# RWKV-7 state update and quick-GELU MLP: another form of the triangular inverse for the first four units

## The chip, the core and the metric

The kernel runs on one core of one Trainium2 chip. The metric is the device time in microseconds of one execution. Five engines work side by side: TensorE (PE in the profile; PEld is its loading of stationary operands), VectorE (DVE), ScalarE (ACT), GpSimd (POOL) and SyncE (SP), which here issues all transfers. Each takes its own instructions in their program order and waits for the others by semaphores.

## The reference

Two blocks follow one another. The first is a recurrence over 768 steps, for 4 batches and 8 heads of 40 channels, with one 40 x 40 state for each batch and head:

```python
for t in range(S):
    y[:, :, t] = np.einsum('bhd,bhde->bhe', rt, state)
    Sa = np.einsum('bhde,bhe->bhd', state, at)
    state_decay = state * wt[:, :, None, :] - np.einsum('bhd,bhe->bhde', Sa, bt)
    state = state_decay + np.einsum('bhd,bhe->bhde', vt, kt)
```

Its output, rearranged to 3072 tokens of 320 values, goes through an MLP: `h = x @ w_in` (320 to 2048), `g = h * sigmoid(1.702 h)`, `g @ w_out` (2048 to 320). All is fp32.

## The kernel before, in words

The 768 steps are cut into 12 chunks of 64 tokens. A unit is one chunk of two of the four batches, 16 batch-heads, so there are 24 units; units 2c and 2c+1 make chunk c. Within a unit the 64 steps become matrix products (`prep`, `inverse`, `solve`), and only the state goes on from unit i to unit i+2. When both units of a chunk are done, the chunk's MLP (`mlp`) can run: 40 groups of ps_up, four activations g, 2 x 8 groups of ps_down, and the stores. The output x of a unit goes to DRAM and back (`part_with`, `get_back`) to be rearranged.

The in-chunk dependence needs T, the inverse of I + N for a strictly triangular 64 x 64 matrix N for each batch-head. `inverse` makes it so. `score_N` computes N in PSUM. The two 32 x 32 diagonal blocks are inverted by five levels of matmuls with a doubling of powers; then two products, ps_Q and ps_T, add the off-diagonal block (`off_one`, `off_two`, with P21, QT and Tc), and T goes into `solve` (ps_X, M, ps_y). Partitions hold two blocks of 64 rows; the four 64 x 64 quarters of TensorE work as independent tiles, and a level is 16 matmuls with a 64 x 64 stationary operand each.

In the form of before a level n has these steps: E (the current power plus the identity, 32 columns for each of eight tiles) is turned by a 32 x 32 transpose on VectorE to ES (L648); ES is spread by a mask `quads` into EX (L655, or in two halves on ScalarE, L653), a block diagonal of two 32 x 32 blocks, which serves as stationary operand; the matmuls multiply EX with W, whose first 32 columns are two times the identity minus E and whose last 32 are the running product; the result is copied to the next W (L684), and two times the identity minus its first half gives the next E (L686). For level 0, E comes from N by two predicated copies onto an identity (L637, one for each diagonal block), and W's first half by a subtraction (L643); the identities in E0 and W0 are set once at the start (L373). After the last level one more transpose and spread make T.

The MLP's weights come as eight pieces of 1280 columns in a 64-bit form: 0 to 3 are w_in, 4 to 7 w_out. Each piece takes a transfer, one ScalarE step (L413) and five VectorE steps (L417, L421, L422, L425, L429). Some are staged in a buffer `extra` of two places, so that piece 4's transfer waits for the end of piece 0, that of 5 for 3, of 6 for 4 and of 7 for 5. ps_up needs pieces 0 to 3; ps_down parts 2k and 2k+1 need piece 4+k.

No loop sets the order of the instructions. Every step is a task of `Plan` with a rank, the engines that may run it with an assumed duration for each, what it reads and writes, and the buffers and PSUM pairs (four, of two banks each) that it takes. `Plan.order` goes through an assumed time line, gives each free engine the able task of the lowest rank, and so decides both engine and place of every instruction; `Plan.paced` does this four times with shifted release times for the MLP's tasks and keeps the order with the earliest assumed end. The tasks are then issued in that order. So a change of some tasks moves many others. MLP tasks have ranks from 10000, units have ranks of ten per unit.

Of the kernel before, what the change touches and what calls it, by code (L numbers as in the profile page):

```python
# [22 lines left out]
ALU = mybir.AluOpType  # L23
ACT = mybir.ActivationFunctionType
# [201 lines left out]
def rwkv7_gelu_quick(ctx: ExitStack, tc: tile.TileContext, time_d, v_d, w_d, wc_d, ak_d, b_d, rv_d, w_in, w_out, out):  # L226
    nc = tc.nc
# [10 lines left out]
    LEVELS = 5  # L238
    WALK = "ebufbub"
    EARLY = 4  # L240
    BY_PE = 4
    ROUNDS, WINDOW, SHARE = 4, 5000.0, 1.0
    RANKS = [14, 16, 20, 24, 35, 37, 39, 41]
    HALF = [slice(0, 64), slice(64, 128)]
    BITS = (0, 1)
# [6 lines left out]
    banks = ctx.enter_context(tc.tile_pool(name="banks", bufs=1, space=bass.MemoryType.PSUM))  # L252

    plan = Plan(dict(logw=3, wc=3, G=1, wch=3, wz=2, time=2, ak=2, b=2, rv=2, FT=3, GT=1, kh=2, bh=2, zr=2, rz=2,
                     A=1, B=1, RV=2, E0=2, W0=2, P21=2, W=2, E=2, ES=2, EX=2, T=2, Tc=1, QT=1, zraw=2, zT=1, M=2, x=1, xT=3, g=4, ob=1), 4)
    tiles, psums, drams = {}, {}, {}

    def single(name, shape):
# [9 lines left out]
    def psum(t, name):  # L268
        if t.pair not in psums:
            psums[t.pair] = banks.tile([128, 2, 512], FP32, tag=f"pair{t.bank}", name=name)  # L270
        return psums[t.pair]

    def mm(o, lhsT, rhs, start):
        nc.tensor.matmul(o, lhsT, rhs, start=start, stop=True, skip_group_check=True)  # L274
# [338 lines left out]
    def turn(i, n, of):  # L613
        return of * 2 * (i // 2) + i % 2 + 2 * n


    def inverse(i):
# [17 lines left out]
        plan.add(R, pe((4, 64)), score_N, reads=T("ahT", "bhT") + ([("preset", 1)] if i == 1 else []), uses=T("ak", "b"), room=T("E0", "P21"), pair=("N", i))  # L635
        for n in BITS:
            plan.add(R, dve(256), lambda t, n=n: nc.vector.copy_predicated(  # L637
                tiles_of(at(E0_t, i)), every(within_of(n), [128, 2, 4, 32]), blocks(psum(t, ""), 64)[:, :, :, 32 * n:32 * n + 32]),
                     writes=T("E0"), pair=("N", i))
        plan.add(R, any2(256), lambda t: copy(t.engine)(  # L640
            at(P21_t, i)[:, :256].rearrange("p (r j t) -> p r j t", r=2, t=32), blocks(psum(t, ""), 64)[:, :, :, :32]),
                 writes=T("P21"), pair=("N", i))
        plan.add(R, {"DVE": 430.0, "POOL": 750.0, "sbuf": True}, lambda t: of(t.engine).tensor_sub(  # L643
            at(W0_t, i)[:, :, :32], two32.unsqueeze(1).to_broadcast([128, 8, 32]), at(E0_t, i)), reads=T("E0"), writes=T("W0"))

        def turned(rank, source, reads, n, dst, writes):

            plan.add(rank, dve(256), lambda t: nc.vector.transpose(ES(n), source(t)), writes=[key("ES", n, 6)], **reads)  # L648

            def spread(t):  # L650
                if t.engine == "ACT":
                    for h in BITS:
                        nc.scalar.activation(dst[:, :, h], ES(n), ACT.Copy, scale=quads[:, h, :1])  # L653
                else:
                    of(t.engine).tensor_mul(dst, ES(n).unsqueeze(2).to_broadcast([128, 8, 2, 32]),  # L655
                                            quads.unsqueeze(1).to_broadcast([128, 8, 2, 32]))
# [12 lines left out]
        def level(n):  # L669
# [18 lines left out]
                     writes=[key("E", n + 1, 5)], pair=pair)  # L688
            turned(rank, lambda t: E(n + 1), dict(reads=[key("E", n + 1, 5)]), n + 1, EX(n + 1), [key("EX", n + 1, 5)])

        for n in range(LEVELS):
# [336 lines left out]
```

## Time and profile before

| | |
|---|---|
| median of 3 runs | 734.87 us (731.48 to 738.36) |
| profiled execution | 741.96 us, its span 740.3 us |
| mean granted TensorE clock | 0.959 |
| PE busy | 679.0 us, 92% of the span |
| DVE busy | 445.9 us, 60% |
| ACT busy | 343.8 us, 46% |
| POOL busy | 214.5 us, 29% |
| moved by DMA | 69.80 MB, mean 94 GB/s |

A line of a group or of the timeline names the engine, the line of the kernel and the operation, then the written and read tiles with their shapes. All matmuls are issued in a helper at L274, so they are told apart by their PSUM tile: ps_level is a level of the inverse, ps_up and ps_down are the MLP. The trace counts each fp32 matmul twice. Times in square brackets are the engine's idle time before the line, with what ended it.

### The profile page before, as it was taken

To read this page: it belongs to the slowest core of one execution; us is meant where nothing else is said; L and a number is where in the kernel's file an instruction comes from. 1 tells how busy PE (TensorE), PEld (TensorE's weight loads), DVE (VectorE), ACT (ScalarE), POOL (GpSimd) and SP (SyncE) were. 2 spreads that over 40 slices of the span, in tenths; PEclk is the share of its full clock that TensorE was granted. 3 is DMA by queue.
4 is the path that set the end of the run, shared out by engine and by line. 5 is a ranking of instruction groups with operands and counts; after the bars stand their busy time and mean duration, and the time that the engine had idled before them with its cause. 6 is when DMAs were issued, how large, how long until landed. Compare 5 with 4: busy or idle time off the path is not lost.

```text
span 740.3 us, 43272 instructions
## 1 busy us (share of the span) xinstructions
PE 679.0 (92%) x20096; PEld 560.7 (76%) x20096; DVE 445.9 (60%) x795; ACT 343.8 (46%) x666; POOL 214.5 (29%) x279
## 2 busy tenths in 40 slices
PE   4575895899999999999999999999999999999997
PEld 3465773687888977887887888988888798777564
DVE  5788798878558566666557467656666546542000
ACT  4555465445535535545645526445446345332120
POOL 7236124243323333322322233422441421200000
PEclk9576699899999999999999999999999999999999
DMA  7951544243251242341332233341331230110000
GB/s 227 350 177 53 168 139 148 65 117 107 57 169 47 77 122 73 87 136 49 99 102 71 74 95 104 98 120 55 99 101 50 83 93 4 40 48 29 13 9 19
DMA packets 31860, 69.80 MB, mean 94 GB/s; under 512 B 5056, under 2 KB 14272, under 8 KB 30656
## 3 DMA queue, kind: packets, MB, share of 16 engines
q1 hardware_dynamic: 31680, 67.03, 30.1%
q8 instruction: 158, 2.59, 1.5%
q14 instruction: 22, 0.18, 0.1%
HBM read 59.15 MB, written 7.86 MB: 91 GB/s over the span
## 4 chain that ended last, share of the span: by engine, by line
PE 77%; DVE 7%; ACT 5%; DMA 5%; issue 2%; POOL 2%; SPq 2%; DVEq 0%; POOLq 0%; ACTq 0%
PE ps_down L274 25%; PE ps_up L274 25%; PE ps_level L274 7%; PE ps_y L274 4%; PE ps_B L274 4%; PE ps_X L274 2%; PE ps_T L274 2%; PE ps_Q L274 2%; DMA ak<-in_ak 1%; PE ps_rz L274 1%; DVE ES L648 1%; PE ps_N L274 1%; PE ps_RV L274 1%; PE ps_A L274 1%; DMA extra<-in_w_out 1%
## 5 line engine op out<-in xcount | busy, mean ns | idle before, releaser
L274 PE MATMUL ps_up<-xT,w_sb 64*64 64x256 f32 x3840 | 251.3, 379 | 2.7 <-DVE RV L605 1.5
L274 PE MATMUL ps_down<-w_sb,g 64*64 64x320 f32 x3072 | 246.6, 436 | 4.9 <-DVE w_sb L429 2.5
L274 PEld LDWEIGHTS ps_up<-xT,w_sb 64*64 64x64 f32 x3840 | 152.7, 134 | 32.0 <-DVE RV L605 1.6
L274 PEld LDWEIGHTS ps_down<-w_sb,g 64*64 64x64 f32 x3072 | 135.6, 135 | 50.3 <-issue 7.6
L274 PEld LDWEIGHTS ps_level<-W,EX 64*64 64x64 f32 x3840 | 85.3, 141 | 41.6 <-ACT EX L653 14.3
L274 PE MATMUL ps_level<-W,EX 64*64 64x64 f32 (+1 forms) x3840 | 87.4, 226 | 26.6 <-ACT EX L653 11.6
L653 ACT ACTIVATE EX<-ES,quads 128x256 f32<-128x256 f32 x120 | 54.5, 501 | 59.7 <-DVE ES L648 57.5
L684 ACT COPY W<-ps_level 128x512 f32<-128x512 f32 x67 | 39.3, 586 | 71.5 <-PE ps_level L274 71.2
L882 ACT ACTIVATE g<-ps_up 128x1024 f32<-128x1024 f32 x48 | 49.1, 1024 | 42.5 <-PE ps_up L274 42.2
L686 DVE TENSOR_TENSOR E<-two,ps_level 128x256 f32<-128x256 f32 x96 | 39.7, 413 | 48.1 <-ACT W L684 48.0
L655 POOL TENSOR_TENSOR EX<-ES,quads 128x512 f32<-128x512 f32 x26 | 37.7, 1449 | 80.3 <-DVE ES L648 57.6
L648 DVE STREAM_TRANSPOSE ES<-E 128x256 f32<-128x256 f32 x120 | 53.2, 444 | 5.6
L582 POOL TENSOR_TENSOR kh<-time,G 128x320 f32<-128x320 f32 x22 | 19.7, 894 | 123.9 <-PE ps_y L274 72.1
L908 DVE TENSOR_TENSOR ob<-ob,ps_down 128x320 f32<-128x320 f32 x24 | 11.6, 485 | 63.4 <-ACT ob L906 63.0
L785 ACT COPY B<-ps_B 128x416 f32<-128x416 f32 x41 | 20.6, 507 | 62.4 <-PE ps_B L274 62.4
L847 POOL TENSOR_TENSOR x<-zr,FT 128x128 f32<-128x128 f32 x80 | 42.7, 563 | 5.4 <-DVE zr L837 3.4
L643 POOL TENSOR_TENSOR W<-two,E 128x256 f32<-128x256 f32 x22 | 16.1, 731 | 95.5 <-DVE E L637 95.5
L274 PE MATMUL ps_y<-M,bh 64*64 64x104 f32 x768 | 36.7, 253 | 0.6 <-issue 0.6
L274 PE MATMUL ps_y<-RV,kh 64*64 64x104 f32 x768 | 36.2, 254 | 0.3 <-DVE M L801 0.3
L574 POOL TENSOR_TENSOR ak<-ak,FT 128x512 f32<-128x512 f32 x18 | 26.9, 1496 | 26.2 <-DMA ak<-in_ak 20.9
L801 DVE TENSOR_TENSOR M<-ps_X,later 128x832 f32<-128x832 f32 x24 | 24.5, 1019 | 15.9 <-PE ps_X L274 15.9
L655 POOL TENSOR_TENSOR T<-ES,quads 128x512 f32<-128x512 f32 x10 | 12.8, 1278 | 71.1 <-DVE ES L648 66.4
(128 smaller groups left out, 1088.2 us busy)
## 6 DMA issues: line engine op xcount, KB each, us to landing
ak<-in_ak SPq DMA_DIRECT2D x48, 160.0 KB
time<-in_time SPq DMA_DIRECT2D x24, 320.0 KB
rv<-in_rv SPq DMA_DIRECT2D x48, 160.0 KB
xT<-x_dram SPq DMA_DIRECT2D x48, 160.0 KB
wc<-in_wc SPq DMA_DIRECT2D x20, 264.0 KB
extra<-in_w_out SPq DMA_DIRECT2D x4, 1280.0 KB
logw<-in_w SPq DMA_DIRECT2D x24, 160.0 KB
b<-in_b SPq DMA_DIRECT2D x48, 80.0 KB
```

The source lines that it names most:

```text
L274: nc.tensor.matmul(o, lhsT, rhs, start=start, stop=True, skip_group_check=True)
L574: plan.add(R, {"DVE": 690.0, "POOL": 1270.0, "sbuf": True}, lambda t: of(t.engine).tensor_mul(ahT(), ahT(), FT_of(i)), reads=T("ak", "FT") ...
L582: plan.add(R + 4, {"POOL": 870.0, "DVE": 490.0, "sbuf": True}, lambda t, n=n, dst=dst: of(t.engine).tensor_mul(dst(i)[:, :, :D], by_head(t ...
L648: plan.add(rank, dve(256), lambda t: nc.vector.transpose(ES(n), source(t)), writes=[key("ES", n, 6)], **reads)
L653: nc.scalar.activation(dst[:, :, h], ES(n), ACT.Copy, scale=quads[:, h, :1])
L655: of(t.engine).tensor_mul(dst, ES(n).unsqueeze(2).to_broadcast([128, 8, 2, 32]), quads.unsqueeze(1).to_broadcast([128, 8, 2, 32]))
L684: plan.add(rank, any2(512), lambda t: copy(t.engine)(tiles_of(W(n + 1)), blocks(psum(t, ""), 64)), writes=[key("W", n + 1, 5)], pair=pair)
L686: plan.add(rank, dve(256), lambda t: nc.vector.tensor_sub(tiles_of(E(n + 1)), every(two32, [128, 2, 4, 32]), blocks(psum(t, ""), 64)[:, :, ...
L785: plan.add(R, any2(416), lambda t: copy(t.engine)(dst(), psum(t, "")[:, :, :208]), writes=[("Bv", i)] if x and c > 0 else T("B"), pair=(na ...
L801: plan.add(R + 1, dve(832), lambda t: nc.vector.tensor_tensor(M_of(i).rearrange("p (j b) n -> p b j n", b=2), psum(t, "")[:, :, :416].rear ...
L847: of(t.engine).tensor_mul(x[:, b ^ u, b], both(i)[:, at, :64], FT_of(i)[:, at])
L882: plan.add(-45, act(1024), lambda t: nc.scalar.activation(g_of(c * NQ + q).rearrange("p m r n -> p r m n"), psum(t, "").rearrange("p r (m ...
```

## The change

A constant PLAIN = 4 divides the units. For units 0 to 3 the levels take another form; from unit 4 on they are as before. E0 and W0 become parts of one tile PT (two buffers), of 96 columns for each of the eight tiles in the new form: 64 of P, 32 of T.

In the new form P is kept as a block diagonal of 64 columns. One multiplication of N in PSUM by the mask `within` makes the first P, in place of the two predicated copies and the subtraction. A transpose of 128 x 512 makes the stationary operand straight from P, as P is a block diagonal already, so that ES and the spread fall away. A level multiplies it with P and T side by side (96 columns; 32 in the last level), and four further matmuls with the identity as stationary operand add the old T to the product in PSUM. The result is copied to PT (768 columns, any of ScalarE and VectorE), and the next stationary operand is transposed straight from PSUM (512 columns, VectorE). The step from the last level to T, and all that follows, stays.

The identity in T's columns is set anew for each of units 0 to 3 by a ScalarE copy; units 4 and 5 set the two places of their form once (ScalarE or VectorE), as PT was used otherwise until then. The presets at the kernel's start fall away.

```diff
+    PLAIN = 4
...
-                     A=1, B=1, RV=2, E0=2, W0=2, P21=2, W=2, ...
+                     A=1, B=1, RV=2, E0=2, W0=2, P21=2, PT=2, W=2, ...
...
-    E0_t, W0_t = several("E0", [128, 8, 32]), several("W0", [128, 8, 64])
-    def preset(engine, n):
-        for t in E0_t[n], W0_t[n][:, :, 32:]:
+    PT_t = several("PT", [128, 8 * 96])
+    E0_t = [t[:, :256].rearrange("p (j t) -> p j t", t=32) for t in PT_t]
+    W0_t = [t[:, 256:].rearrange("p (j t) -> p j t", t=64) for t in PT_t]
+
+    def preset(engine, *places):
+        for t in places:
             copy(engine)(t, one32.unsqueeze(1).to_broadcast([128, 8, 32]))
-    preset("ACT", 0)
-    plan.add(-8, {"ACT": 800.0, "DVE": 900.0}, lambda t: preset(t.engine, 1), writes=[("preset", 1)])
...
+        PT = at(PT_t, i).rearrange("p (j t) -> p j t", t=96)
+        if i < PLAIN:
+            plan.add(R - 3, {"ACT": 400.0}, lambda t: preset(t.engine, PT[:, :, 64:]), room=T("PT"), writes=T("preset"))
+        elif i < PLAIN + 2:
+            plan.add(R - 3, {"ACT": 800.0, "DVE": 900.0}, lambda t: preset(t.engine, at(E0_t, i), at(W0_t, i)[:, :, 32:]), room=T("PT"),
+                     writes=T("preset"))
...
-        for n in BITS:
+        for n in BITS if i >= PLAIN else ():
             plan.add(R, dve(256), lambda t, n=n: nc.vector.copy_predicated(
...
-        plan.add(R, {"DVE": 430.0, "POOL": 750.0, "sbuf": True}, lambda t: of(t.engine).tensor_sub(
-            at(W0_t, i)[:, :, :32], two32.unsqueeze(1).to_broadcast([128, 8, 32]), at(E0_t, i)), reads=T("E0"), writes=T("W0"))
+        if i >= PLAIN:
+            plan.add(R, {"DVE": 430.0, "POOL": 750.0, "sbuf": True}, lambda t: of(t.engine).tensor_sub(
+                at(W0_t, i)[:, :, :32], two32.unsqueeze(1).to_broadcast([128, 8, 32]), at(E0_t, i)), reads=T("E0"), writes=T("W0"))
...
-        turned(R, lambda t: at(E0_t, i), dict(reads=T("E0")), 0, EX(0), [key("EX", 0, 5)])
+        if i >= PLAIN:
+            turned(R, lambda t: at(E0_t, i), dict(reads=T("E0")), 0, EX(0), [key("EX", 0, 5)])
+        else:
+            plan.add(R, dve(512), lambda t: nc.vector.tensor_tensor(
+                tiles_of(PT)[:, :, :, :64], blocks(psum(t, ""), 64), every(within.rearrange("p n t -> p (n t)"), [128, 2, 4, 64]), ALU.mult),
+                     writes=[("PV", turn(i, 0, 5))], pair=("N", i))
+
+        square = lambda n: EX(n).rearrange("p j n t -> p j (n t)")
+
+        def turned_square(source, reads, n):
+            plan.add(R + 0.5 * n, dve(512), lambda t: nc.vector.transpose(
+                square(n) if "pair" not in reads else tiles_of(square(n)), source(t)), writes=[key("EX", n, 5)], **reads)
+        if i < PLAIN:
+            turned_square(lambda t: PT[:, :, :64], dict(reads=[("PV", turn(i, 0, 5))]), 0)
...
+        def plain_level(n):
+            last = n == LEVELS - 1
+            wide, rank = 32 if last else 96, R + 0.5 + 0.5 * n
+
+            def go(t):
+                ps, x = psum(t, "ps_level"), square(n)
+                for k in range(4):
+                    for r, q in QUARTERS:
+                        mm(ps[HALF[q], r, k * wide:(k + 1) * wide], x[HALF[r], index(n, r, q, k)],
+                           PT[HALF[r], index(n, r, q, k), 96 - wide:], k == 0)
+                for r, q in QUARTERS:
...
+                    mm(ps[HALF[q], r, :4 * wide].rearrange("p (a b t) -> p a b t", a=2, b=2)[:, :, :, wide - 32:], ident[HALF[r]], got, False)
+            pair = ("L", turn(i, n, 5))
+            plan.add(rank, pe((4, wide), (1, 128)), go, reads=[key("EX", n, 5), ("PV", turn(i, n, 5))], uses=T("PT"),
+                     room=T("T", "Tc") if last else [], pair=pair)
+            if last:
+                return pair
+            plan.add(rank, any2(768), lambda t: copy(t.engine)(tiles_of(PT), blocks(psum(t, ""), 96)),
+                     writes=[("PV", turn(i, n + 1, 5))], pair=pair)
+            turned_square(lambda t: blocks(psum(t, ""), 96)[:, :, :, :64], dict(pair=pair), n + 1)
+
         for n in range(LEVELS):
-            pair = level(n)
+            pair = plain_level(n) if i < PLAIN else level(n)
```

More of the change, by code (lines that the diff above doesn't have):

```diff
@@ L254, in rwkv7_gelu_quick @@
     plan = Plan(dict(logw=3, wc=3, G=1, wch=3, wz=2, time=2, ak=2, b=2, rv=2, FT=3, GT=1, kh=2, bh=2, zr=2, rz=2,
-                     A=1, B=1, RV=2, E0=2, W0=2, P21=2, W=2, E=2, ES=2, EX=2, T=2, Tc=1, QT=1, zraw=2, zT=1, M=2, x=1, xT=3, g=4, ob=1), 4)
+                     A=1, B=1, RV=2, E0=2, W0=2, P21=2, PT=2, W=2, E=2, ES=2, EX=2, T=2, Tc=1, QT=1, zraw=2, zT=1, M=2, x=1, xT=3, g=4, ob=1), 4)
     tiles, psums, drams = {}, {}, {}
@@ L634, in score_N @@
                     mm(ps[HALF[b], e, o:o + 64], ahT()[HALF[e], j], b_of(i)[HALF[e], j], o == 0)
-        plan.add(R, pe((4, 64)), score_N, reads=T("ahT", "bhT") + ([("preset", 1)] if i == 1 else []), uses=T("ak", "b"), room=T("E0", "P21"), pair=("N", i))
-        for n in BITS:
+        plan.add(R, pe((4, 64)), score_N, reads=T("ahT", "bhT") + (T("preset") if i < PLAIN + 2 else []), uses=T("ak", "b"), room=T("E0", "P21"), pair=("N", i))
+        for n in BITS if i >= PLAIN else ():
             plan.add(R, dve(256), lambda t, n=n: nc.vector.copy_predicated(
@@ L689, in level @@
             turned(rank, lambda t: E(n + 1), dict(reads=[key("E", n + 1, 5)]), n + 1, EX(n + 1), [key("EX", n + 1, 5)])
+        def plain_level(n):
[8 more added lines that the diff above has]
+                for r, q in QUARTERS:
+                    first, hi, lo = index(n, r, q, 0), index(n, r, q, 2) - index(n, r, q, 0), index(n, r, q, 1) - index(n, r, q, 0)
+                    of_k = PT[HALF[r], :, 64:].rearrange("p (a b c) t -> p a b c t", a=2, b=2)
+                    bits = {4: 0, 2: 1, 1: 2}
+                    fixed = 7 - hi - lo
+                    picks = [slice(None)] * 5
+                    picks[1 + bits[fixed]] = int(bool(first & fixed))
+                    got = of_k[tuple(picks)]
+                    if hi < lo:
+                        got = got.rearrange("p a b t -> p b a t")
+                    mm(ps[HALF[q], r, :4 * wide].rearrange("p (a b t) -> p a b t", a=2, b=2)[:, :, :, wide - 32:], ident[HALF[r]], got, False)
[7 more added lines that the diff above has]
+            turned_square(lambda t: blocks(psum(t, ""), 96)[:, :, :, :64], dict(pair=pair), n + 1)
         for n in range(LEVELS):
-            pair = level(n)
+            pair = plain_level(n) if i < PLAIN else level(n)
         turned(R + 3, lambda t: blocks(psum(t, ""), 32), dict(pair=pair), 5, at(T_t, i), T("T0"))
```

## The prediction

> **What bounds the kernel now.** I read the 40 slices first, to see when TensorE is full and at which clock.
>
> ```profile
> PE   4575895899999999999999999999999999999997
> DVE  5788798878558566666557467656666546542000
> PEclk9576699899999999999999999999999999999999
> ```
>
> A slice is 18.5 us. From the ninth on, PE is at nine tenths and at full clock until the end; before that it is half idle, some slices at 0.5 to 0.7 of the clock, while DVE is at 7 to 9 tenths. So there are two regimes. Then the stretches of 20 us, whose columns are length, then busy us and instruction count of PE, weight load, DVE, ACT and POOL, then clock, DMA share and GB/s:
>
> ```profile
> 20.00:40.00 20.00, 9.05 (x306) 7.73 (x299) 16.53 (x30) 12.93 (x31) 3.22 (x3) 0.59 0.90 326
> 60.00:80.00 20.00, 14.13 (x444) 13.13 (x440) 16.23 (x23) 10.08 (x21) 8.92 (x8) 0.59 0.23 62
> 120.00:140.00 20.00, 14.37 (x408) 9.74 (x404) 17.78 (x26) 10.99 (x24) 6.87 (x6) 0.76 0.08 19
> 240.00:700.00 460.00, 452.99 (x13684) 376.61 (x13680) 262.65 (x499) 213.03 (x399) 126.78 (x157) 1.00 0.27 77
> ```
>
> Over the first nine such stretches PE is busy 131.4 of 180 us: 48.6 us idle, and what is busy at clock 0.59 takes longer besides. From 240 to 700 it idles 7 us. Every microsecond by which the front ends sooner should reach the end, and every microsecond of TensorE work added after the front costs itself. Who is waited for in the front: PE's own waits up to 80 us, in total us, times, longest.
>
> ```profile
> PE ps_level L274 <- POOL EX L655: 7.6, 3, 3.4
> PE ps_RV L274 <- DMA rv<-in_rv: 6.6, 2, 3.4
> PE ps_level L274 <- ACT EX L653: 6.5, 4, 3.2
> ```
>
> 14.1 us wait for EX, the stationary operand that one inversion level makes for the next. One such round in the timeline (start, duration, then the idle time before it):
>
> ```profile
> 22.84 1.13 PE L274 MATMUL ps_level<-W,EX 64*64 64x64 f32 x32 [2.61 <-ACT EX L653]
> ...
> 24.04 0.59 ACT L684 COPY W<-ps_level 128x512 f32<-128x512 f32 x1 [0.89 <-PE ps_level L274]
> ...
> 24.66 0.42 DVE L686 TENSOR_TENSOR E<-two,ps_level 128x256 f32<-128x256 f32 x1 [1.90 <-ACT W L684]
> ...
> 25.11 0.45 DVE L648 STREAM_TRANSPOSE ES<-E 128x256 f32<-128x256 f32 x1
> ...
> 26.46 0.91 ACT L653 ACTIVATE EX<-ES,quads 128x256 f32<-128x256 f32 x2
> ...
> 27.42 0.69 PE L274 MATMUL ps_level<-W,EX 64*64 64x64 f32 x32 [0.27 <-ACT EX L653]
> ```
>
> 4.6 us from level to level, of which 0.69 to 1.13 are the matmuls (the trace counts each of the 16 twice). Two later marks of the same timeline: the first MLP matmul (ps_up) starts at 81.32, and ps_down stands from 129.4 to 131.70 for weight piece 6, whose last step is on DVE:
>
> ```profile
> 131.70 4.54 PE L274 MATMUL ps_down<-w_sb,g 64*64 64x320 f32 x32 [2.31 <-DVE w_sb L429]
> ```
>
> **What the Trainium skill says.** "PSUM — Partial Sum Buffer", PSUM bank collisions: no two engines may touch one bank and quadrant at once, two readers included. The trace agrees: E on DVE stands 1.90 us until W on ACT is out of the same PSUM. So the new copy and the new transpose, which read one PSUM pair, come one after the other. "TensorE: Matmul & The Clock Gate", Part 1: idle windows drop the clock to half. The round above at 1.13 us, against 0.46 from start to start at 101.7 us, agrees in kind.
>
> **The change, part by part.** Prices first. The transpose of 128x512 isn't in the trace: 128x256 takes 0.445, and an elementwise DVE step goes from 0.41 at 256 to 0.69 at 512, so I add 0.28: 0.72. "Vector Engine (DVE) Microarchitecture Reference", The reshape front-end, gives one element per cycle and lane, which asks for no more; bounds 0.6 (no second start-up, faster stream) and 1.0 (twice 0.445 and some). The 768-wide copy lies between W (0.59 at 512) and g (1.02 at 1024) on ACT: 0.80; on DVE between 0.69 (512) and 1.02 (832): 0.95. Sixteen level matmuls of 96 columns lie between 0.46 (64 columns) and 0.71 (104, ps_B): 0.66; four identity matmuls of 128 columns between 0.18 (ps_y, 104) and 0.28 (ps_cum, 160): 0.22.
>
> Removed per unit: two predicated copies (0.91), five transposes of 256 (2.2), four subtractions for E (1.65), all DVE; one subtraction for W0 (0.73 POOL); five spreads to EX (0.91 ACT, 0.69 DVE or 1.3 to 1.5 POOL); four W copies (0.59). Added: one mask multiply (0.70), five transposes of 512 (3.6), four copies of 768, one preset copy (0.40 ACT). DVE saves 0.5 per unit by this, and more because its spreads and most copies go. Summing the DVE orders of both programs with durations from the trace: up to the last step of weight pieces 0 to 7 before takes 26, 46, 55, 62, 79, 87, 102 and 112 us of DVE work, the changed one 26, 40, 52, 59, 74, 82, 89 and 104.
>
> A level's round becomes matmuls 0.88, copy 0.80, transpose 0.72: 2.4 plus hops, against 0.46 to 1.13 + 0.59 + 0.42 + 0.45 + 0.91 = 2.8 to 3.5 plus three more hand-overs. Two of those go, and each handed-over step queued behind weight work on ACT or POOL.
>
> TensorE pays 0.42 for each of 16 levels and 0.22 for 4 last ones: 7.6 us. Units 0 to 2 do it before the MLP starts, where PE idles; unit 3's 1.9 us lie among ps_up. If the idle cover weren't there, all 7.6 would count. The presets of units 4 and 5 (0.80 each) sit on ACT ahead of T's spread, once each: at most 1.6, taken as hidden, since T there waits for DVE as well. The wait added is that of the transpose for the copy's PSUM (or the reverse). Queued behind it on DVE are weight steps, for which ps_down waits; and the transposes themselves stand behind weight steps of 0.8 to 2.5.
>
> Now the walk along the new order, with these durations, cold matmuls (1.1 to 1.7 a group) until the MLP runs, each engine in order. Level 0 of unit 0 now stands ahead of unit 1's ps_RV, which waited for a DMA until 17.9. Before, then mine:
> - level 1 of unit 0: 22.8, 19.2 (behind that ps_RV).
> - T of unit 0 done on DVE: 43.5, 42.2. Little, because piece 1's three DVE steps now stand ahead of it.
> - T of unit 1: start 62.4, 53.5; its M: 64.7, 57.9; y, x on POOL, the transfer to DRAM and back as before (7.7 us from issue to ps_up): first ps_up 81.3, 74.
> - piece 3: 81.2, 74. y of unit 2: 89.5, 89.5: nothing, as 60 ps_up groups now stand ahead of its second off-diagonal product.
> - piece 4: 103.8, 94 (its DVE steps come right behind piece 3). Level 0 of unit 3: 101.5, 91.
> - piece 6: 131.7, 112.5. Its transfer waits for piece 4's end, and took 8.3 us; 94 + 8.3 + ACT and DVE 8 fits.
> - T of unit 3: 138.4, 121; its y: 142.2, 126; piece 7: 144.1, 128.
> - first ps_up of chunk 1: 163.4, 141, with unit 4's old-style levels as the last chain.
>
> My walk has few stalls. It gives 128 us for 104 of DVE work (1.23), where before took 144.1 for 112.0 (1.29). At before's ratio piece 7 ends at 134, so I put 5 on the last mark: 146, a gain of 17.
>
> At that mark the two orders aren't equally far. Counting matmul groups by warm start-to-start times, 544.0 of TensorE work are in before and 551.5 in the changed program; 80.0 and 83.6 are done at the mark, 464.0 and 467.9 are left. Before takes 740.3 - 163.4 = 577 for 464: 1.24 each. 3.9 more are 4.8 us. Net 17.4 - 4.8 = 12.6, call it 13. The tail is alike: after the last ps_y 39.7 and 40.6 of work.
>
> The profiled execution took 741.96 (span 740.3, 1.7 around it), 1% above the median of 734.87. 741.96 - 13 = 729; the same 13 off the median is **722**.
>
> **Rivals.**
> 1. *The weights set the front.* DVE's 0.9 share and the chained transfers through the staging buffer keep pieces 4 to 7 where they are, and only the first ps_up moves by 7. For it: the ps_down wait above and 7.0 us in which ACT waited for that transfer. Against: DVE work up to piece 6 falls by 12.5. Then 7 - 4.8 = 2 remain: 733.
> 2. *Slower: TensorE's added columns.* TensorE is the bound for 560 us. If the front isn't shortened at all, because the orders put ps_up ahead of unit 2's T and unit 3's transposes behind piece 6 on DVE, then the 7.6 us at 1.24 are 9.4: 744. It exceeds 1% once the first ps_up of chunk 1 comes after 163.4 + 7.3 - 4.8 = 166. Against it: TensorE idles 48.6 us ahead of that.
> 3. *My walk is right without the discount, and fewer cold matmuls help:* 22 - 4.8 = 17.6, with 5 of clock 23: 712.
>
> **How the numbers follow.** 1% (about what a measurement of this kernel tells from no change) is 727.5 and 742.2. Forecast 0.46, rival 3 0.18, rival 1 0.22, rival 2 0.14. Rival 3 and most of the forecast lie under 727.5: 0.62 faster; rival 1 with the forecast's upper edge within: 0.23; slower 0.15. The transposes' bounds (0.6 to 1.0, 20 of them, half on the path) are -1 and +3, and a rearranged order after the front may shift stalls by a few us either way. The range runs from rival 3 less 3 to just short of rival 2: 709 to 739, leaving 0.05 below and 0.15 above.
>
> **What would show it.** Right: first ps_up near 74 to 77, ps_down not waiting at 130, first ps_up of chunk 1 near 146, PE idle before 180 lower by 10 or more, ps_level busy up by some 7 us, no EX waits in the first 70 us. Wrong: a 512 transpose near 1 us, copies on ACT standing behind weight steps, DVE still at nine tenths with pieces 6 and 7 at 130 and 143, or new idle slices after 200.

## The result, and the profile after

| | before | after |
|---|---|---|
| median | 736.01 us (731.48 to 738.44, 19 runs) | 729.44 us (727.0 to 732.38, 19 runs) |
| ratio | | 0.9918, interval 0.9899 to 0.9937 |
| profiled execution, span | 741.96, 740.3 us | 732.38, 730.7 us |
| mean TensorE clock | 0.959 | 0.981 |
| DVE, ACT, POOL busy | 445.9, 343.8, 214.5 us | 426.6, 352.8, 211.1 us |

The change saves 6.6 us, 0.8%. The forecast was 13 us, so the direction held and half of the gain is missing. The slices of the profile after:

```profile
PE   4575998998999999999999999999999999999997
...
DVE  6569798965665656656664655647566666431000
...
PEclk9869999999999999999999999999999999999999
```

A slice is 18.3 us here. TensorE is now at eight tenths or more from the fifth slice on (before: from the eighth), and its clock at nine tenths or more from the fourth (before: from the sixth). The stretches of 20 us that the prediction showed, with one more, in the same columns:

```profile
20.00:40.00 20.00, 11.41 (x320) 10.41 (x317) 12.38 (x15) 8.79 (x21) 1.47 (x2) 0.78 0.91 323
60.00:80.00 20.00, 12.91 (x445) 11.34 (x449) 18.88 (x24) 8.02 (x24) 9.07 (x9) 0.91 0.38 116
120.00:140.00 20.00, 16.10 (x540) 12.98 (x544) 17.90 (x28) 8.11 (x18) 8.79 (x9) 0.91 0.32 94
160.00:180.00 20.00, 16.20 (x516) 12.64 (x512) 11.80 (x23) 15.69 (x27) 5.39 (x5) 1.00 0.23 67
240.00:700.00 460.00, 455.88 (x13576) 373.66 (x13572) 251.78 (x476) 217.77 (x409) 129.70 (x159) 1.00 0.26 77
```

From 160 to 180 us PE is busy 16.20 of 20: behind the front there is a hole that the kernel before didn't have, neither at that time (the line below) nor as far behind its own first ps_up of chunk 1, where from 176 to 196 us it is busy all of the 20 us:

```profile
160.00:180.00 20.00, 18.54 (x587) 15.79 (x582) 14.86 (x27) 12.86 (x22) 8.83 (x9) 1.00 0.40 117
```

That first ps_up in before and after:

```profile
163.37 0.39 PE L274 MATMUL ps_up<-xT,w_sb 64*64 64x256 f32 x3
...
147.08 1.50 PE L275 MATMUL ps_up<-xT,w_sb 64*64 64x256 f32 x24
```

The marks of the two timelines, beside the forecast for each:

| start, us | before | forecast | after |
|---|---|---|---|
| T of unit 0 done on DVE | 43.5 | 42.2 | 48.3 |
| y of unit 0 | 48.0 | not given | 52.5 |
| first ps_up | 81.3 | 74 | 75.1 |
| y of unit 2 | 89.5 | 89.5 | 91.5 |
| piece 6 done | 131.7 | 112.5 | 114.1 |
| y of unit 3 | 142.2 | 126 | 127.8 |
| piece 7 done | 144.0 | 128, discounted to 134 | 131.6 |
| first ps_up of chunk 1 ("the mark") | 163.4 | 146 | 147.1 |
| from the mark to the end of the span | 576.9 | 581.7 | 583.6 |

So the front came out as forecast, 16.3 us shorter at the mark against 17.4. ps_down, which waited 2.31 us for piece 6 at 131.7, waits 1.35 for piece 7 at the same time:

```profile
129.54 2.10 DVE L432 TENSOR_TENSOR w_sb<-w_sb,extra 128x1280 f32<-128x1280 f32 x1
...
131.69 1.31 PE L275 MATMUL ps_down<-w_sb,g 64*64 64x320 f32 x16 [1.35 <-DVE w_sb L432]
```

A round of the new form, in the timeline of after (start, duration, idle time before):

```profile
41.40 0.80 ACT L741 COPY PT<-ps_level 128x768 f32<-128x768 f32 x1
...
42.23 0.72 DVE L680 STREAM_TRANSPOSE EX<-ps_level 128x512 f32<-128x512 f32 x1 [1.49 <-ACT PT L741]
...
43.00 1.56 PE L275 MATMUL ps_level<-PT,EX 64*64 64x96 f32 x32 [2.73 <-DVE EX L680]
...
44.33 0.65 PE L275 MATMUL ps_level<-PT,ident 64*64 64x128 f32 x8
...
45.40 0.80 ACT L741 COPY PT<-ps_level 128x768 f32<-128x768 f32 x1 [2.40 <-PE ps_level L275]
```

4.0 us from copy to copy with a cold clock, of which 2.0 are matmuls; the 128x512 transpose takes 0.72 and the 768-wide copy 0.80, both as priced. The waits of PE up to 80 us:

```profile
PE ps_level L275 <- DVE EX L680: 6.4, 4, 2.7
PE ps_RV L275 <- DMA rv<-in_rv: 5.4, 3, 4.1
PE ps_level L275 <- issue: 5.0, 2, 3.0
...
PE ps_A L275 <- issue: 3.2, 1, 3.2
```

The EX waits fell from 14.1 to 6.4 us. In their place stand 8.2 us of "issue": TensorE waits for nothing that the profile shows. That unit 0 got later and not earlier I put down to these pauses; the experiments test it.

What has to be explained: a front 16.3 us shorter, of which 6.7 were given back behind the mark in these two traces, and a median that moved by less than the traces' 9.6.

### The profile page after: what moved, and what is told of

Read it like the earlier page. It is cut to its first block, busy times and chain, and to the rows that moved or that the text cites. A ratio compares the mean times of both kernels' runs of the same rounds, so it can differ in the third digit from the quotient of the medians.

```text
span 730.7 us, 43534 instructions
## 1 busy us (share of the span) xinstructions
PE 679.2 (93%) x20256; PEld 557.8 (76%) x20256; DVE 426.6 (58%) x747; ACT 352.8 (48%) x672; POOL 211.1 (29%) x281
## 4 chain that ended last, share of the span: by engine, by line
PE 83%; DVE 5%; issue 4%; ACT 4%; POOL 2%; DMA 2%; SPq 0%; POOLq 0%; ACTq 0%; DVEq 0%
PE ps_down L275 27%; PE ps_up L275 27%; PE ps_level L275 8%; PE ps_B L275 5%; PE ps_y L275 4%; PE ps_X L275 3%; PE ps_Q L275 2%; PE ps_T L275 1%; PE ps_rz L275 1%; PE ps_A L275 1%; PE ps_N L275 1%; PE ps_zT L275 1%; PE ps_RV L275 1%; DVE w_sb L432 1%; DMA rv<-in_rv 1%
## 5 line engine op out<-in xcount | busy, mean ns | idle before, releaser
L275 PE MATMUL ps_down<-w_sb,g 64*64 64x320 f32 x3072 | 240.1, 431 | 2.4 <-DVE w_sb L432 1.9
L275 PEld LDWEIGHTS ps_up<-xT,w_sb 64*64 64x64 f32 x3840 | 160.4, 134 | 33.9 <-issue 6.7
L275 PEld LDWEIGHTS ps_down<-w_sb,g 64*64 64x64 f32 x3072 | 126.6, 133 | 49.3 <-DVE w_sb L432 2.2
L936 ACT ACTIVATE g<-ps_up 128x1024 f32<-128x1024 f32 x48 | 49.2, 1024 | 48.8 <-PE ps_up L275 48.6
L585 POOL TENSOR_TENSOR kh<-time,G 128x320 f32<-128x320 f32 x24 | 21.8, 909 | 168.1 <-PE ps_y L275 89.9
L664 ACT ACTIVATE EX<-ES,quads 128x256 f32<-128x256 f32 x102 | 46.2, 501 | 47.3 <-DVE ES L659 46.9
L275 PEld LDWEIGHTS ps_level<-W,EX 64*64 64x64 f32 x2560 | 57.0, 134 | 11.2 <-issue 2.3
L275 PE MATMUL ps_level<-W,EX 64*64 64x64 f32 (+1 forms) x2560 | 56.9, 219 | 0.5 <-ACT EX L664 0.4
L275 PE MATMUL ps_level<-PT,EX 64*64 64x64 f32 (+2 forms) x1280 | 35.5, 246 | 14.5 <-DVE EX L680 6.8
L275 PEld LDWEIGHTS ps_level<-PT,EX 64*64 64x64 f32 x1280 | 32.8, 146 | 20.6 <-issue 9.4
L659 DVE STREAM_TRANSPOSE ES<-E 128x256 f32<-128x256 f32 x80 | 35.6, 445 | 4.3
L666 POOL TENSOR_TENSOR EX<-ES,quads 128x512 f32<-128x512 f32 x19 | 26.7, 1404 | 23.6 <-DVE ES L659 16.7
```

What stands on the lines that cost most here:

```text
L585: plan.add(R + 4, {"POOL": 870.0, "DVE": 490.0, "sbuf": True}, lambda t, n=n, dst=dst: of(t.engine).tensor_mul(dst(i)[:, :, :D], by_head(t ...
L936: plan.add(-45, act(1024), lambda t: nc.scalar.activation(g_of(c * NQ + q).rearrange("p m r n -> p r m n"), psum(t, "").rearrange("p r (m ...
```

## Experiments

My first theory was that the rest of the gain is lost in the later part by the chance of one written-out order, beside 3 us of added TensorE work; the rivals were that the first trace of before misled me about the front, that the new form itself costs time later on, and that the new form's own parts cost more than priced. "The mark" is the first ps_up of chunk 1 throughout, and each ratio is to the kernel before in the same comparison.

**Both kernels once more**, unchanged. 

> The kernel before, profiled a second time: is the first profiled execution (741.96 us, where 19 executions have the median 736.0 and reach 738.4) a typical one? If it is not, a second trace has a span of some 733 to 737 us, and its front is shorter: first ps_up of chunk 1 some 3 to 5 us ahead of 163.4, with the rest as in the first trace (577 us from that mark to the end). If the front is always the same and the profiled execution lost its time later, the mark stays at 163 and the part after it is shorter. Time against itself: ratio 1.00, within 0.3%.

> The changed kernel, profiled a second time. Its first profiled execution took 732.38 us, the median of 19 is 729.4. Ratio 0.992. If the TensorE gaps at 23, 30 and 37 us of the first trace (3.2, 3.0, 2.0 us in the middle of a group, nothing waited for) belong to the program and not to that execution, they come again at the same instructions, and y of unit 0 again comes near 52.5, behind the 48.0 of before. If they are chance, y of unit 0 comes near 47.

Before: 734.96 us, ratio 1.0007 (0.9993 to 1.0022), span 733.1. After: 730.47, ratio 0.9939 (0.9907 to 0.997), span 728.7. The new trace of before has the same front as the first (first ps_up 79.8, mark 163.0, y of unit 3 at 142.2 in both) and is 7 us shorter behind it: 570.1 from the mark to the end against 576.9. After repeats its front too (mark 147.2, gaps at the same instructions) and takes 581.5. So the traced execution of before that I subtracted from was a long one of its kernel, above all the 19 timed runs of the first comparison, and it was long in the late part. With the second pair the front gains 15.8 and the later part gives back 11.4; 4.4 remain.

**Without the identity products**, the order kept:

```diff
                         mm(ps[HALF[q], r, k * wide:(k + 1) * wide], x[HALF[r], index(n, r, q, k)],
                            PT[HALF[r], index(n, r, q, k), 96 - wide:], k == 0)
-                for r, q in QUARTERS:
...
-                    mm(ps[HALF[q], r, :4 * wide].rearrange("p (a b t) -> p a b t", a=2, b=2)[:, :, :, wide - 32:], ident[HALF[r]], got, False)
```

> The changed kernel without the identity products in the levels of units 0 to 3 (the old T is not added, so T is not the inverse); the assumed durations are kept, so that all other instructions stay where they are. 20 groups of four matmuls fall away, 4.4 us of warm TensorE time. If their price is TensorE time alone, hidden where TensorE idles, only unit 3's five groups lie behind the first ps_up: 1 to 1.5 us less than the changed kernel, 728. If TensorE is short of instructions in the front (256 instructions each 7 us between 20 and 40 us, as the gaps of the first trace suggest), the 16 instructions that each group saves bring y of unit 0 forward by 3 to 4 us, the gaps between 20 and 40 us fall from 8.2 us to 5 or less, and the end comes 3 to 5 us earlier: 725.

725.5 us (six executions), ratio 0.9877 (0.9842 to 0.9912), as the second expectation has it: 4 to 5 us under the changed kernel, where the products' warm time is 4.3 us of TensorE, all of it ahead of the mark, where TensorE has idle time. y of unit 0 comes at 48.5 (4.0 earlier), the first ps_up at 71.2, the mark at 141.5, and 580.0 follow: the 5.6 us gained at the mark pass on to the end whole. "Issue" waits between 15 and 45 us fall from 8.2 to 4.7.

**The same products idle in the kernel before**: four identity matmuls more in each level of units 0 to 3, into columns that nobody reads (`i` is the unit).

```diff
+                if i < 4:
+                    for r, q in QUARTERS:
+                        mm(ps[HALF[q], r, 384:512], ident[HALF[r]], w[HALF[r], 0:2].rearrange("p j t -> p (j t)"), False)
```

> The kernel before with four further matmuls in each level of units 0 to 3: identity as stationary operand, 128 columns of W, into PSUM columns that nobody reads; the result and the order of all instructions stay as before. It prices the added TensorE work by itself, 4.4 us warm and 320 instructions. If TensorE's idle time in the front hides it: within 1 us of before, at most 1.5 for those of unit 3. If it is paid in full as rival 2 of the prediction has it: 4.4 to 5.5 us slower, 0.7%.

737.73 us, ratio 1.0035 (1.0016 to 1.0054), 2.6 us: first ps_up at 84.0, mark at 164.3. Both expectations missed: the products are neither hidden nor paid in full, and cheaper here than in the changed kernel, whose gaps they lengthen.

**Thin transfers.** In the trace of after, TensorE's gaps in the first 45 us are these three:

```profile
23.21 0.34 PE L275 MATMUL ps_A<-ak 64*64 64x64 f32 x6 [3.21 <-issue]
...
30.26 0.64 PE L275 MATMUL ps_level<-PT,EX 64*64 64x96 f32 x20 [2.98 <-issue]
...
37.61 0.37 PE L275 MATMUL ps_level<-PT,EX 64*64 64x32 f32 x12 [2.01 <-issue]
```

All three stand inside a group of matmuls whose first ones had run, 254 and 256 instructions of TensorE apart (matmuls and weight loads as the trace records them); the second trace has 2.48, 3.73 and 1.85 at the same instructions. The DMA view of 18 to 45 us has a queue whose kind is "instruction", with packets of 16 KB (packets, MB, share):

```profile
q8 instruction: 4, 0.07, 0.9%
```

The start times of these packets tie the gaps to them: packets start at 20.66, 27.73 and 35.02 us, and TensorE goes on 2.55, 2.54 and 2.59 us later. It is so everywhere. From 12 to 60 us the eighteen traces of this case have 43 pauses on "issue" of more than 0.4 us, and each ends 2.3 to 2.9 us after such a packet's start. The next run makes the kernel's own transfers smaller: of weight pieces 0 to 3 it moves a quarter and leaves the rest out of the result.

```diff
+    for at, big, eng in (0, extra, nc.vector), (4, w_sb, nc.gpsimd), (6, w_sb, nc.gpsimd), (2, extra, nc.vector):
+        eng.memset(big[:, at * PIECE + PIECE // 2:(at + 2) * PIECE], 0.0)
...
-        plan.add(rank, {"SP": 350.0}, lambda t: nc.sync.dma_start(raw(), src), ...
+        plan.add(rank, {"SP": 350.0}, lambda t: nc.sync.dma_start(raw()[:, :PIECE // 4] if n < 4 else raw(), src[:, :PIECE // 4] if n < 4 else src), ...
```

> The changed kernel with the transfers of weight pieces 0 to 3 cut to a quarter (the rest of the staged words is set to zero, so those weights are left out of the result): 3.9 MB less is moved in the first 50 us, the instructions of TensorE stay as they are. If TensorE's gaps of 2 to 3.7 us at 22, 30 and 37 us, in which it waits for nothing the profile shows, come from its instructions arriving late behind those transfers, they fall below 1 us each, and y of unit 0 comes at 45 to 48 in place of 52. If they come from something in TensorE's own order they stay, at the same instructions.

One execution: 728.04 us, first ps_up 68.3, mark 140.9, y of unit 0 at 45.7, 6.8 us earlier. The waits of PE from 15 to 45 us, its stretch from 20 to 40 us, and the instruction packets from 18 to 45 us:

```profile
PE ps_level L275 <- DVE EX L682: 6.2, 5, 2.3
PE ps_level L275 <- issue: 1.0, 1, 1.0
...
PE ps_A L275 <- issue: 0.7, 1, 0.7
```

```profile
20.00:40.00 20.00, 12.58 (x476) 11.00 (x472) 16.30 (x22) 13.72 (x29) 2.13 (x3) 0.87 0.73 235
```

```profile
q8 instruction: 6, 0.10, 1.5%
```

The gaps are 1.0 or less, six instruction packets arrive where four did, and 476 matmul records run where 320 did. So TensorE stood for its instructions, and they came late behind the kernel's own transfers. Part of the earlier mark is due to weights that arrive earlier; that part wasn't separated. The mark's 6.2 us don't reach the end: 585.4 us follow it, some 2 to 4 more than in the changed kernel, and why is open.

**Later transfers**, with everything computed:

```diff
         before = [("weight", m) for m in range(n) if raws[m] == at]
+        before += {2: [("rebased", 0)], 3: [("rebased", 1)]}.get(n, [])
```

> The changed kernel with the transfer of piece 2 held until piece 0's ScalarE step and that of piece 3 until piece 1's, so that fewer bytes are under way from 17 to 35 us; nothing is left out. With the first four transfers thinned, the gaps of TensorE at 22, 30 and 37 us went and y of unit 0 came 6.8 us earlier. If it is the number of bytes under way at that time, the gaps shrink to 1 to 2 us each, y of unit 0 comes at 47 to 50, and the time falls to 723 to 729 (the order moves too, by some 3 us). If the same bytes later do the same harm, or pieces 2 and 3 now come late, the time is 729 to 736.

735.2 us, ratio 0.996 (0.9936 to 0.9983). The "issue" waits from 15 to 45 us halve to 4.1 and y of unit 0 comes at 49.6, as the first theory has it; but the order moved too, piece 7 is done at 136.1 in place of 131.6 and the mark is at 151.5. The time is that of the second expectation. From 25 to 35 us its transfers move 246 GB/s, where the two traces of after move 316 and 292, and the third gap is gone, so fewer bytes there go with shorter gaps; the kernel as ordered can't use it. But the rate alone doesn't decide: from 35 to 45 us the held transfers run at 398 GB/s, and TensorE, which waits for EX in that stretch, has no pause on "issue" above 0.4 us.

**Stationaries from SBUF**: the transpose reads the copy in place of PSUM.

```diff
-            turned_square(lambda t: blocks(psum(t, ""), 96)[:, :, :, :64], dict(pair=pair), n + 1)
+            turned_square(lambda t: PT[:, :, :64], dict(reads=[("PV", turn(i, n + 1, 5))]), n + 1)
```

> The changed kernel with the next stationary operand transposed from the copy in SBUF (after it) in place of straight from PSUM beside it. If the two readers of one PSUM pair come one after the other anyway, the round of a level stays the same to 0.2 us, the first ps_up at 75 +-1, and the time at 727 to 733 (the order moves a little). If the transpose straight from PSUM ran beside the copy or ahead of it, a level grows by up to 0.8 us, units 0 and 1 (ten levels, partly beside one another) by 4 to 8, and the time goes to 733 to 738.

733.94 us, ratio 0.9952 (0.9921 to 0.9983). The level's hand-over in this kernel:

```profile
20.35 0.80 ACT L741 COPY PT<-ps_level 128x768 f32<-128x768 f32 x1 [3.78 <-PE ps_level L275]
...
21.18 0.71 DVE L680 STREAM_TRANSPOSE EX<-PT 128x512 f32<-128x512 f32 x1 [0.41 <-ACT PT L741]
```

and the same one in the changed kernel:

```profile
19.71 0.80 ACT L741 COPY PT<-ps_level 128x768 f32<-128x768 f32 x1 [3.77 <-PE ps_level L275]
...
20.54 0.72 DVE L680 STREAM_TRANSPOSE EX<-ps_level 128x512 f32<-128x512 f32 x1 [0.99 <-ACT PT L741]
```

0.83 us from the start of the copy to that of the transpose, either way. Straight from PSUM it waits for the copy all the same, as the prediction took from the Trainium skill ("PSUM — Partial Sum Buffer", PSUM bank collisions). What it waits for is ScalarE's semaphore, so the program keeps the two readers apart; what the chip would do with both at once no run shows. The source of the transpose is worth nothing in a level. The time lies above the expected 727 to 733 by 1, and the first ps_up at 78.1 in place of 75 +-1: other steps stand in another order (mark 151.4, then 581.2). At 105.0 and 116.0 us, ahead of the mark, this order has two more pauses for instructions, of 2.35 and 2.57 us; the changed kernel's largest between 60 us and its mark is 1.03. As the levels are alike, I put the difference down to the order, which is an argument and not shown.

**How many units have the new form**: `PLAIN = 2` and `PLAIN = 8`.

> PLAIN at 2: the new form for units 0 and 1 alone, 3.8 us less TensorE work than with four units. If the gain of the front comes from all four units, the first ps_up stays near 75 and the mark comes back to 152 to 157; 730 to 734. If units 2 and 3 bring nothing by their form (the weights set their times), the mark stays at 147 to 149 and the time falls by the work left out: 724 to 728.

737.36 us, ratio 1.0012 (0.9991 to 1.0032), outside both expectations. First ps_up 80.3, mark 158.7. With two units, in the one order that was run, nearly nothing of the gain is there, though the chains of units 0 and 1, which lead to the first ps_up, have the new form: y of unit 1 comes at 66.7 (65.8 in before, 63.4 with four). Steps of units 2 and 3 lie in the same queues ahead of the first ps_up, and I take it that their smaller VectorE work counts there too; which steps those are wasn't separated.

> PLAIN at 8: the new form for units 4 to 7 as well, 7.6 us more TensorE work, nearly all of it behind the first ps_up of chunk 1, where TensorE is at nine tenths and more. If that stretch only pays for work, the front stays as with four units (mark 147) and the end moves by +6 to +8: 735 to 738. If the shorter chain of a level helps there too (levels still waited for between 147 and 240 us), the time stays at 728 to 732.

739.88 us, ratio 1.0023 (0.9999 to 1.0046). Mark 145.6, then 590.4: 7.8 more than the 582.6 (mean of two) of the changed kernel, for 7.5 us of added work. Some 6 us of this work lie behind the mark. That is the first expectation: where TensorE is full, the new form pays for its columns and shows no gain. It is one order of each; the next part shows what orders do.

**Other orders of the same work.** `WINDOW` shifts the planner's release times for the MLP's tasks. With another value both kernels keep at least the first 80 groups of TensorE, and the rest stands in another order, some steps on another engine.

```diff
-    ROUNDS, WINDOW, SHARE = 4, 5000.0, 1.0
+    ROUNDS, WINDOW, SHARE = 4, 4000.0, 1.0
```

> The changed kernel with the planner's WINDOW at 4000 in place of 5000: the same work, the same order of TensorE for about the first 80 us, another order behind that. The traces so far show the front 15.8 to 16.3 us shorter than before, and 6.7 to 11.4 us given back behind the mark (first ps_up of chunk 1), 3.2 of them as TensorE work. Theory A (the rest is the chance of this one order): the stretch from the mark to the end, 581.5 to 583.6 in the changed kernel, moves by several us with the order, and can come down to 574 to 578, so 722 to 727 in all; the first ps_up stays at 75 +-1. Theory B (the new form itself costs the later part, whatever the order): the stretch stays at 581 to 584 for a mark near 147, and the time at 728 to 733.

> The kernel before with WINDOW at 4000, another order of its same work behind the first 80 us. Theory A: the stretch from the mark to the end, 570.1 and 577 in its two traces, moves with the order by several us either way (568 to 583), and the time with it: 730 to 742. Theory B: the stretch stays at 570 to 577, the time at 732 to 737, and the difference to the changed kernel at WINDOW 4000 is again about 6.

> The kernel before with WINDOW at 6000, a third order of its same work. Theory A: the three orders of the kernel before differ by more than 3 us among each other in the stretch from the mark to the end, so that a difference of 6 us between two programs holds a good part of chance. Theory B: they agree within 2 us.

> The changed kernel with WINDOW at 7000, a third order of its work (the three orders of the kernel before took 735.0, 741.1 and 746.3, two of the changed kernel 729.4 and 730.2). If the time is a matter of a few us by order for both forms, this one lies anywhere from 725 to 740, and the stretch from the mark to the end at 575 to 588. If the changed kernel hardly depends on the order, it lies at 728 to 732.

> A fourth order of the changed kernel. If the forms differ by the sum's 11 to 13 us in the mean over orders and each order scatters by some 3 to 5 about its form's mean, this one lies at 726 to 737, with the first ps_up of chunk 1 at 146 to 150. Otherwise (the pair's 6 is the form's true gain) the mean of the changed orders stays within 6 of that of before.

> A fourth order of the kernel before. If its order at 5000 was a lucky one, this lies at 738 to 746, mark at 159 to 164 and 574 to 585 from there to the end. If the two slower orders were unlucky ones, it lies at 733 to 738.

> A fifth order of the kernel before, with the same two expectations: 738 to 746 if 5000 was lucky, 733 to 738 if 4000 and 6000 were unlucky.

| kernel, WINDOW | median us | ratio | mark | mark to end |
|---|---|---|---|---|
| before, 5000 | 734.96 | 1 | 163.0, 163.4 | 570.1, 576.9 |
| before, 4000 | 746.27 | 1.011 (1.0066 to 1.0153) | 159.6 | 584.9 |
| before, 5500 | 740.0 | 1.0039 (1.0016 to 1.0062) | 160.1 | 580.7 |
| before, 6000 | 741.07 | 1.0049 (1.003 to 1.0068) | 159.8 | 579.0 |
| before, 10000 | 743.07 | 1.0053 (1.0022 to 1.0084) | 162.2 | 578.9 |
| after, 5000 | 729.44, 730.47 | 0.9918, 0.9939 | 147.1, 147.2 | 583.6, 581.5 |
| after, 3000 | 727.14 | 0.9842 (0.9798 to 0.9885) | 145.8 | 581.6 |
| after, 4000 | 730.2 | 0.9881 (0.982 to 0.9942) | 149.6 | 583.1 |
| after, 7000 | 735.66 | 0.9964 (0.9946 to 0.9982) | 147.7 | 587.2 |

The kernel before took 735.2 to 737.9 in these comparisons, so the ratios are to be read, not the medians. The rows at 4000 and 3000 rest on four executions each, the others on 10 to 20; each mark and stretch is of one trace, and two traces of one order differ by up to 6.8 us in the stretch.

Of the expectations, those of the kernel before at 6000 (theory A) and of the changed one at 7000 (a matter of order) came true. The changed one at 4000 came out nearer theory B (583.1 from the mark, 730.2 in all, but the mark at 149.6), and the kernel before at 4000 slower than either theory. At 3000 the time fell within the first expectation and the mark 0.2 us ahead of it. The two that were to tell a lucky order, at 5500 and 10000, are 737.8 and 738.9 when the ratio is put on the 735.0 of before: at the border between the two expectations, so that only the intervals of the ratios decide.

The order of before that the comparison rests on is the fastest of its five: all four others are slower by 0.4 to 1.1%, with intervals clear of 1. It has the latest mark of the five and the shortest way from there: over the orders the mark comes at 161.0 in the mean before and at 147.6 after, 13.4 apart and not 16, so part of what the pair gains at the mark and loses behind it is the standing order's own. The changed kernel's four orders lie between 0.984 and 0.996. The means of the two forms are 1.0050 and 0.9904 (the two ratios at 5000 counted as one), 1.46% apart, 10.8 us. The scatter of the orders, 0.39% over five and 0.53% over four, gives this difference a standard error of 0.32% (the root of 0.39²/5 + 0.53²/4), 2.4 us. So both the pair's 6 and the sum's 13 lie within what orders do; that the form's own gain is nearer 11 is likely, and not more than that. Theory B, that the new form costs the later part 7 to 11 us whatever the order, isn't borne out, though its lower end isn't excluded: the mean stretch from mark to end is 579.4 and 583.6, 4.2 apart with a standard error of 2.2 by the same reckoning, and 3.2 of them are work.

What the late part loses isn't one place. I summed the pauses behind the mark in which a matmul's start comes over 0.3 us later than the warm start-to-start time of its predecessor's width: 9.3 us in 9 pauses (second trace of before), 13.3 in 15 (first trace), 18.7 in 26 (before at 4000), 15.5 and 14.8 in 21 (after, both traces), 21.8 in 31 (after at 7000). The other five orders have 14.2 to 16.1, so it is the standing order of before that has the fewest. One of them in after is at 169.9, in the hole shown above: ps_rz stands 1.49 us for zT, which ScalarE copies only after a g and two table loads of 1.28 us each:

```profile
169.43 0.41 ACT L806 COPY zT<-ps_zT 128x320 f32<-128x320 f32 x1
...
169.89 0.69 PE L275 MATMUL ps_rz<-rv,zT 64*64 64x64 f32 x32 [1.49 <-ACT zT L806]
```

From the second trace of before to that of after the pauses grow by 5.5 us and the work by 3.1, 8.6 of the 11.4 given back; the rest isn't found in pauses above 0.3 us.

## Why the prediction was right in direction and wrong in size

The step that failed is the one behind the mark. The prediction let the stretch from the first ps_up of chunk 1 to the end grow by the added TensorE work alone, 4.8 us, put nothing for the rearranged order, and took its 13 off the median as if the traced execution were typical there. The second pair of traces, whose executions are near the medians, shows 11.4 us lost in that stretch. The front came out 15.8 to 16.3 us shorter, close to the 17.4. The steps, as it put them:

- *The front "half idle", and the round of 1.13 us against 0.46.* Two readings were loose. TensorE idles 48.6 of 180 us there, 27%. And 1.13 is the length of a group, 0.46 a time from start to start; the group at 101.53 us takes 0.64, against 1.13 cold.
- *The walk along the new order, first ps_up 74, y of unit 3 126, mark 141, discounted to 146.* From the first ps_up on, the rows of the table are right within 2.5 us with the discount (pieces 3 and 4, at 77.9 for 74 and 96.6 for 94, were further off). The early ones were wrong: T of unit 0 at 48.3 and not 42.2, T of unit 1 started at 58.4 and not 53.5. Nothing in the walk had a TensorE that stands without instructions, 8.2 us in all. The kernel before hid this: it stood for EX at the same time, and its only such wait in the first 60 us was 0.6 us. That the mark came within 1.1 us of 146 is in part luck: the 5 us of discount were taken from the ratio of time to VectorE work, and they covered pauses that the walk didn't have. Where the pauses shrink, the mark comes at 140.9 (thin transfers, with earlier weights) and 141.5 (no identity products), the walk's own 141.
- *Prices.* Transpose 0.71 to 0.72 for 0.72, copy 0.80 on ACT and 0.96 on DVE for 0.80 and 0.95. The added TensorE work is 7.4 us for 7.6.
- *The identity products, 0.22 a group, idle cover in the front.* In TensorE time right (4.3 us in all), in effect too small: 4 to 5 us on the whole kernel, where most were taken as hidden. The cover failed too: in the changed front TensorE lacks instructions, and every instruction more is fetched.
- *1.24 for each microsecond of work left, 4.8 us.* The count was wrong: I took the 320 columns of ps_down, and the 32 of ps_Q, ps_T and the last level, at the start-to-start time of 128 and 64. Counted by width from the warm starts (0.068 us at 320, 0.0138 at 32) the work is 638.5 and 645.9, of which 83.8 and 88.1 are done at the mark and 554.7 and 557.8 are left. 576.9 for 554.7 is 1.04. The term is 3.1 x 1.04 = 3.2 in place of 4.8, and rival 2's full price 7.7 in place of 9.4. Put right alone, it makes the forecast 14, further off.
- *"The same 13 off the median".* This is one half of the step that failed. The profiled execution was 1% above the median, and I took the excess to leave the difference as it is. It lay in the late part, which the forecast left as it was: 576.9 there, 570.1 in the second trace. Counted from the second trace, the later part loses 11.4 and not 6.7.
- *"A rearranged order after the front may shift stalls by a few us either way", and nothing for it in the likeliest case.* This is the other half. The size was about right, but it went into the range and not into the sum: the order that stood there was the best of the five that were run, and the new one gave 11.4 back behind the mark where the sum had 4.8. With the front's 15.8 for 17.4 that is the whole way from 12.6 to the 4.4 of the second pair, and most of the way to the 6.6 and 4.5 between the medians of the two pairs. That it is the order and not the form rests on the table of orders, with the error given there.

Of the rivals, 1 (weights set the front, 733) and 2 (added columns decide, 744) were wrong about the front; 3 (712) too, since its mark of 141 came at 147.1. The measured 729 is the forecast's mechanism, with half of its gain given back behind the front.

The marks it named: first ps_up at 75.1, within 74 to 77; the mark at 147.1 for 146; no EX waits in the first 70 us was too much to ask (4.7 us, for 10.9 in before); PE idle before 180 us fell by 7.3 in the first pair of traces and by 10.9 in the second, where 10 or more was forecast. The clock there rose in both (third last column; before, before again, after, after again):

```profile
0.00:180.00 180.00, 131.37 (x4000) 109.47 (x4004) 142.98 (x222) 97.32 (x205) 70.73 (x102) 0.83 0.49 158
0.00:180.00 180.00, 128.78 (x4004) 107.79 (x4008) 143.55 (x222) 97.34 (x205) 71.44 (x102) 0.86 0.48 158
...
0.00:180.00 180.00, 138.73 (x4428) 119.33 (x4432) 136.26 (x198) 100.58 (x202) 62.72 (x98) 0.92 0.49 160
0.00:180.00 180.00, 139.68 (x4428) 119.39 (x4432) 136.57 (x198) 100.54 (x202) 63.39 (x98) 0.91 0.49 160
```

How much of the front's gain is the clock and how much less idle time wasn't separated.

The fastest kernel that computes everything is the changed one with WINDOW at 3000, 727.14 us over four executions, ratio 0.9842.

## What to carry to other kernels

Where a planner writes out the order, a change of a few tasks reshuffles the whole program: measure several orders of both forms before putting 1% down to the form, and reckon with a standing order that is a lucky one (here the best of five). Take the trace's own marks for the stage that you shorten, but check with a second trace whether the other stages are typical before subtracting from the median. In these runs the shorter chain paid where TensorE had idle time, and its added matmuls cost about their full time where it was full (eight units against four).

## What the hardware showed that was not expected

TensorE can stand for its own instructions. The profile shows such a pause as a wait on "issue", and in the changed front it falls in the middle of a group of matmuls. The instructions come as DMA packets of 16 KB, and the pauses end 2.3 to 2.9 us after such a packet starts, in all 43 cases from 12 to 60 us of the eighteen traces.

With 308 to 323 GB/s of other transfers under way (20 to 40 us, both traces of after) TensorE paused 1.9 to 3.7 us about every 255 instructions, and with 235 GB/s (thin transfers, one execution) at most 1.0 us. That is no threshold: with 398 GB/s there was no such pause while TensorE waited for EX (later transfers), and at 116 us, behind 209 GB/s from 110 to 116, there was one of 2.57 us (stationaries from SBUF). What delays a packet was not found beyond that. The kernel without the identity products agrees: a fifth fewer matmuls in a level, and 3.5 us less of such waits.
